# Gated attention and mixer: tokens permuted for longer reads, weights spread over batch 0, all score blocks of batch 0 computed, z doubled on chip

## The chip, the cores and the metric

The kernel runs on one core of one Trainium2 chip. The metric is the device time of one execution in microseconds (us). An execution is called fast or slow by its time against the fastest of the same kernel; all comparisons below are between fast runs. PE is the tensor engine, DVE the vector engine, ACT the scalar engine, POOL the GpSimd engine (it also issues the loads from memory here), and SP issues the DMA transposes and the stores. A line such as L116 is the line of the kernel that the profile belongs to; the same statement has another number in each kernel.

## The reference

Eight batches of 3008 tokens with 256 channels; z has 64 channels.

```python
scores = (1.0 / S) * np.matmul(z, z.transpose(0, 2, 1))
attn = np.maximum(scores, 0.0) ** 2
x = u * np.matmul(attn, v)                                   # first unit
h = np.maximum(x.transpose(0, 2, 1) @ w_tok1, 0.0) @ w_tok2  # second unit: mixer over tokens
y = x + h.transpose(0, 2, 1)
out = y + np.maximum(y @ w_ch1, 0.0) @ w_ch2                 # and over channels
```

## The kernel before

Tokens are cut in six blocks of 512 (the last has 448). For each batch there are six rows (blocks q of queries) of six groups (blocks g of keys): 36 groups. Scores are symmetric, so a block with g > q is computed once and transposed by a DMA ("flipped", tile `fl`) to serve as block (g, q). The mixer of a batch is cut in pieces that fill PE during the attention of the next batch; during batch 0 there are no such pieces, so batch 0 shows every wait.

Each engine runs its instructions in the order of the program. These are the parts that matter:

```python
def load_z(b, zT, c):            # two loads, one for each half of zr, then a transpose
    zr = sb.tile([P, GK, 2, d_qk], BF16, tag="zr", bufs=2)
    for h in range(2):
        nc.gpsimd.dma_start(out=zr[:, :t1 - t0, h, :], in_=z[b, t0 * P:t1 * P, :]
                            .rearrange("(t p) d -> p t d", p=P))
    ...                          # (the tail is cut)
    nc.sync.dma_start_transpose(out=zT[:, t0:t0 + GK, :], in_=...)

def load_uT(b, q):               # one load on POOL's queue, one transpose on SP's
    ...
# the start: z and v of batch 0, then
load_uT(0, 0)
load_weights()                   # all four weights in five DMAs
load_uT(0, 1)

def scores(b, q, g):
    ...                          # 4 matmuls; relu on ACT (rl), square on DVE (at, 3 buffers)
    if flip:                     # g > q
        fl = sb.tile([P, GK, QW], BF16, tag="fl", bufs=10)
        nc.sync.dma_start_transpose(out=fl..., in_=at[:])
        attn[b, g, q] = fl

for n, (b, q, g) in enumerate(groups):
    for f in fetch.get(n, []):   # loads put at group n
        f()
    if g >= q:
        scores(*directs[ahead])  # one computed block ahead
    ...                          # 8 matmuls of block g with v, gate with u at the end of the row
```

## Time and profile before

| stage (us from the start) | length | PE busy | granted clock |
|---|---|---|---|
| until the first scores, 0 to 9.4 | 9.4 | 0 | 1.00 |
| row 0 of batch 0, 9.4 to 74.5 | 65.1 | 22.1 | 0.90, 0.50, 0.79 |
| rows 1 to 5 of batch 0, 74.5 to 142.45 | 67.95 | 64.14 | 0.95 |
| batches 1 to 7 and the last mixer | 1123.95 | 1099.69 | 1.00 |

The whole is 1266.06 us (median of three runs, 1265.81 to 1267.21); the profiled span is 1266.4 us. The three clock figures of row 0 belong to its part before the empty stretch, to that stretch, and to its part after. The stages are told apart in the timeline of PE: a row begins with the 64-row matmuls of the tail block, which wait for the gate of the row before ("PE acc <- DVE xT"). The lines themselves are in the prediction.

### The profile page before, as it was taken

To read this page: it belongs to the slowest core of one execution; us is meant where nothing else is said; L and a number is where in the kernel's file an instruction comes from. 1 tells how busy PE (TensorE), PEld (TensorE's weight loads), DVE (VectorE), ACT (ScalarE), POOL (GpSimd) and SP (SyncE) were. 2 spreads that over 40 slices of the span, in tenths; PEclk is the share of its full clock that TensorE was granted. 3 is DMA by queue.
4 is the path that set the end of the run, shared out by engine and by line. 5 is a ranking of instruction groups with operands and counts; after the bars stand their busy time and mean duration, and the time that the engine had idled before them with its cause. 6 is when DMAs were issued, how large, how long until landed. Compare 5 with 4: busy or idle time off the path is not lost.

```text
span 1266.4 us, 17085 instructions
## 1 busy us (share of the span) xinstructions
PE 1185.9 (94%) x6929; PEld 623.5 (49%) x7008; DVE 578.1 (46%) x744; ACT 472.2 (37%) x489; POOL 174.7 (14%) x258
## 2 busy tenths in 40 slices
PE   4079989999999999999999999999999999999998
PEld 1023444555455645455455554555455554555566
DVE  1043355444644355534644436543554436444444
ACT  3044334334343144433434343432443334442122
POOL 7112301102120200203011020201102010000000
PEclk9589999999999999999999999999999999999999
DMA  9999998949798697959979497895979588553122
GB/s 114 196 183 174 167 151 144 157 81 173 130 146 148 97 169 136 151 104 138 168 123 159 92 166 137 139 164 87 174 124 163 100 138 148 111 116 84 32 74 67
DMA packets 560223, 168.60 MB, mean 133 GB/s; under 512 B 482384, under 2 KB 559632, under 8 KB 560144
## 3 DMA queue, kind: packets, MB, share of 16 engines
q1 hardware_dynamic: 453504, 131.64, 56.0%
q0 software_dynamic: 106640, 35.86, 26.9%
q8 instruction: 55, 0.90, 0.3%
q14 instruction: 24, 0.20, 0.1%
HBM read 71.70 MB, written 24.64 MB: 76 GB/s over the span
## 4 chain that ended last, share of the span: by engine, by line
PE 80%; DMA 7%; DVE 6%; issue 3%; ACT 2%; POOL 1%; SPq 0%; DVEq 0%; ACTq 0%; POOLq 0%
PE acc L212 34%; PE op L319 20%; PE hp L301 17%; PE sc L159 5%; DMA fl<-at 4%; PE a_ps L266 3%; DVE xT L284 3%; DMA ur<-in_u_dram 2%; ACT rl L172 2%; DVE h2pre L306 1%; DVE at L176 1%; DVE xT L238 1%; DMA zr<-in_z_dram 1%; DMA zT<-zr 0%; PE h_ps L280 0%
## 5 line engine op out<-in xcount | busy, mean ns | idle before, releaser
L172 ACT ACTIVATE rl<-sc 128x1024 bf16<-128x1024 f32 x336 | 324.2, 1016 | 451.8 <-PE sc L159 422.5
L212 PE MATMUL acc<-at,v_sb 128*128 128x512 bf16 (+1 forms) x1337 | 337.5, 385 | 45.3 <-DVE at L176 32.6
L212 PEld LDWEIGHTS <-v_sb 128*128 128x128 bf16 (+1 forms) x2304 | 210.2, 98 | 323.6 <-issue 123.8
L176 DVE TENSOR_TENSOR at<-rl 128x1024 bf16<-128x1024 bf16 x240 | 165.5, 692 | 271.7 <-ACT rl L172 206.6
L319 PE MATMUL op<-w_ch_sb,h2pre 128*128 128x256 bf16 (+1 forms) x2304 | 279.1, 273 | 1.1
L301 PE MATMUL hp<-xT,w_ch_sb 128*128 128x512 bf16 (+1 forms) x1120 | 272.0, 374 | 2.6 <-DVE xT L284 0.2
L319 PEld LDWEIGHTS <-h2pre 128*128 128x128 bf16 (+1 forms) x2304 | 224.2, 98 | 62.2 <-ACT h2pre L308 6.3
L308 ACT ACTIVATE h2pre<-hp 128x1024 bf16<-128x1024 f32 (+1 forms) x144 | 144.9, 1006 | 281.6 <-PE hp L301 263.9
L212 PE MATMUL acc<-fl,v_sb 128*128 128x512 bf16 (+1 forms) x921 | 223.8, 370 | 2.2 <-issue 0.2
L306 DVE TENSOR_SCALAR h2pre<-hp 128x1024 bf16<-128x1024 f32 (+1 forms) x144 | 172.6, 1200 | 79.6 <-PE hp L301 79.5
L301 PEld LDWEIGHTS <-w_ch_sb 128*128 128x128 bf16 x1152 | 112.6, 98 | 131.4 <-issue 4.4
L73 POOL DMA_DIRECT2D zr<-in_z_dram x96 | 72.3, 759 | 454.9 <-DMA zT<-zr 453.6
L327 DVE TENSOR_TENSOR res<-op,u_sb 128x512 f32<-128x512 f32 x88 | 60.7, 689 | 156.3 <-PE op L319 150.5
L159 PE MATMUL sc<-zT 64*128 64x512 bf16 (+1 forms) x672 | 105.4, 385 | 23.8 <-DMA zT<-zr 21.7
L178 DVE TENSOR_TENSOR at<-rl 128x1024 bf16<-128x1024 bf16 (+1 forms) x96 | 64.3, 680 | 76.5 <-ACT rl L172 71.1
L238 DVE TENSOR_TENSOR xT<-acc,uT 128x512 bf16<-128x512 f32 (+1 forms) x96 | 61.8, 665 | 71.7 <-PE acc L212 71.2
L88 POOL DMA_DIRECT2D v_sb<-in_v_dram x48 | 36.3, 762 | 366.3 <-PE acc L212 359.7
L159 PEld LDWEIGHTS <-zT 64*128 64x128 bf16 x672 | 20.5, 94 | 88.9 <-issue 60.5
L284 DVE TENSOR_TENSOR xT<-xT,h_ps 128x1024 bf16<-128x1024 bf16 (+1 forms) x48 | 53.9, 1193 | 22.4 <-PE h_ps L280 22.4
L100 POOL DMA_DIRECT2D ur<-in_u_dram x48 | 36.2, 754 | 69.0 <-DMA uT<-ur 65.9
L280 PE MATMUL h_ps<-w_tok_sb,a_sb 128*128 128x512 bf16 (+1 forms) x191 | 43.2, 374 | 1.6 <-ACT a_sb L272 0.7
L266 PE MATMUL a_ps<-x_sb,w_tok_sb 128*128 128x256 bf16 x384 | 44.4, 273 | 0.0
(21 smaller groups left out, 104.2 us busy)
## 6 DMA issues: line engine op xcount, KB each, us to landing
out_dram<-res SPq DMA_DIRECT2D x88, 256.0 KB, 2.5
v_sb<-in_v_dram POOLq DMA_DIRECT2D x40, 256.0 KB, 4.7
ur<-in_u_dram POOLq DMA_DIRECT2D x40, 256.0 KB, 5.5
zr<-in_z_dram POOLq DMA_DIRECT2D x80, 64.0 KB, 4.5
fl<-at SPq DMA_TRANSPOSE x120, 4.8
v_sb<-in_v_dram POOLq DMA_DIRECT2D x8, 192.0 KB, 8.2
w_ch_sb<-in_moe_w_ch_dram POOLq DMA_DIRECT2D x2, 768.0 KB, 26.1
ur<-in_u_dram POOLq DMA_DIRECT2D x8, 192.0 KB, 6.0
```

Of the source, the lines that this page charges most:

```text
L73: nc.gpsimd.dma_start(out=zr[:, : t1 - t0, h, :], in_=z[b, t0 * P:t1 * P, :].rearrange("(t p) d -> p t d", p=P))
L159: nc.tensor.matmul(sc[:, r, :W], zT[h, k * P:(k + 1) * P], zT[h, q * QW:q * QW + W], start=True, stop=True)
L172: nc.scalar.activation(rl[:, :, :W], sc[:, :, :W], ACT.Relu, scale=inv_S)
L176: nc.vector.tensor_mul(a4[:, :, pair, :], r4, r4)
L212: nc.tensor.matmul(o, vt[rows, i, dh * P:(dh + 1) * P], rhs, start=st, stop=sp, skip_group_check=True)
L238: nc.vector.tensor_mul(xT[:, dh, :full * P].rearrange("p (t s) -> p t s", s=P), acc[:, :full * P].rearrange("p (t s) -> p t s", s=P), uT[: ...
L266: nc.tensor.matmul(st["a_ps"][:, th, :], w_tok1_sb[:, k, th * P:(th + 1) * P], x[:, :, i, :], start=(k == 0 and th == 0), stop=(k == KT - ...
L284: nc.vector.tensor_add(xT[:, :, :W], xT[:, :, :W], h[:, :, :W])
L301: nc.tensor.matmul(hp[:, r, :W], w_ch1_sb[:, dc, cc * P:(cc + 1) * P], xT[:, dc, :W], start=(dc == 0), stop=(dc == DT - 1))
L306: nc.vector.tensor_single_scalar(h2[:, :, :W], hp[:, :, :W], 0.0, AX.max)
L308: nc.scalar.activation(h2[:, :, :W], hp[:, :, :W], ACT.Relu)
L319: nc.tensor.matmul(op[:rows[i], i, :], st["h2", q, cc // 2][:, cc % 2, c0:c0 + rows[i]], w_ch2_sb[:, cc, :], start=(cc == 0 and i == 0), s ...
```

## The change

Its intent: fewer and longer pieces in the loads (a partition reads four rows in one piece), no block of weights in front of u, no flips during batch 0 where DMA is the bottleneck, and half the loads of z. z of the later batches is also asked for later (from group 18 of the batch before theirs instead of from group 7) and doubled on POOL; this isn't printed here. The core of the change (comments and the changes of layout cut):

```diff
+    def rows_of(ap, c):
+        return ap[c * QW:c * QW + n * P, :].rearrange("(p t) d -> p t d", t=n)
-    def load_z(b, zT, c):  ...two loads into zr, transpose
+    def load_z(b, c):
+        zs = sb.tile([P, GK, d_qk], BF16, tag="zs", name="zs", bufs=6)
+        nc.gpsimd.dma_start(out=zs[:, :n, :], in_=rows_of(z[b], c))
+    def turn_z(zs, zT, c, engine):
+        zr = sb.tile([P, GK, 2, d_qk], BF16, tag="zr", name="zr", bufs=2)
+        engine.tensor_copy(zr[:], zs.unsqueeze(2).to_broadcast([P, GK, 2, d_qk]))
+        nc.sync.dma_start_transpose(out=zT[:, c * GK:c * GK + GK, :], in_=...)
 ...
+    def direct_block(b, q, g):
+        return b == 0 or g >= q
-        flip = g > q
+        flip = g > q and b > 0
 ...
-    load_uT(0, 0)
-    load_weights()
-    load_uT(0, 1)
+    for j, c in enumerate(vorder):
+        zs0[c] = load_z(0, c)
+        load_v(0, c)
+        if j == 2:
+            load_uT(0, 0)
 ...
+    at_group(4, lambda: load_uT(0, 1))
+    for c in range(NG):
+        at_group(NG + 1 + 4 * c, lambda c=c: load_w_tok1(c))
+        at_group(NG + 3 + 4 * c, lambda c=c: load_w_tok2(c))   # staged, reordered on POOL
+    for part in range(4):
+        at_group(2 * NG + 6 * part, lambda part=part: load_w_ch(part))
+    turn_z(zs0[vorder[0]], zTs[0], vorder[0], nc.vector)
     scores(*directs[0])
 ...
+        if n + 1 < NG:
+            c = groups[n + 1][2]
+            turn_z(zs0[c], zTs[0], c, nc.vector)
-        if g >= q and ahead < len(directs):
+        if direct_block(b, q, g) and ahead < len(directs):
             scores(*directs[ahead])
```

More of the change, by code (lines that the diff above doesn't have):

```diff
@@ L64, with last_rows @@
     w_ch2_sb = consts.tile([P, CHT, D], BF16)
-    def load_z(b, zT, c):
-        t0, t1 = c * GK, min(c * GK + GK, KT - 1)
-        zr = sb.tile([P, GK, 2, d_qk], BF16, tag="zr", name="zr", bufs=2)
-        for h in range(2):
-            nc.gpsimd.dma_start(
-                out=zr[:, : t1 - t0, h, :],
-                in_=z[b, t0 * P:t1 * P, :].rearrange("(t p) d -> p t d", p=P))
-        if t1 - t0 < GK:
+    full_tiles = [w // P for w in widths]
+    def rows_of(ap, c):
+        n = full_tiles[c]
+        return ap[c * QW:c * QW + n * P, :].rearrange("(p t) d -> p t d", t=n)
+    def last_rows(ap):
+        return ap[(KT - 1) * P:, :]
+    def load_z(b, c):
+        zs = sb.tile([P, GK, d_qk], BF16, tag="zs", name="zs", bufs=6)
+        n = full_tiles[c]
+        nc.gpsimd.dma_start(out=zs[:, :n, :], in_=rows_of(z[b], c))
+        if n < GK:
             for r in range(2):
                 nc.gpsimd.dma_start(
-                    out=zr[r * TAIL:(r + 1) * TAIL, GK - 1],
-                    in_=z[b, (KT - 1) * P:, :].unsqueeze(1)
-                    .to_broadcast([TAIL, 2, d_qk]))
+                    out=zs[r * TAIL:(r + 1) * TAIL, n, :], in_=last_rows(z[b]))
+        return zs
+    def turn_z(zs, zT, c, engine):
+        zr = sb.tile([P, GK, 2, d_qk], BF16, tag="zr", name="zr", bufs=2)
+        engine.tensor_copy(zr[:], zs.unsqueeze(2).to_broadcast([P, GK, 2, d_qk]))
         nc.sync.dma_start_transpose(
-            out=zT[:, t0:t0 + GK, :], in_=zr.rearrange("p t h d -> p (t h d)"))
+            out=zT[:, c * GK:c * GK + GK, :], in_=zr.rearrange("p t h d -> p (t h d)"))
     def load_v(b, c):
         vt = sb.tile([P, GK, D], BF16, tag="v", name="v_sb", bufs=8)
-        t0, t1 = c * GK, min(c * GK + GK, KT - 1)
-        nc.gpsimd.dma_start(
-            out=vt[:, : t1 - t0, :],
-            in_=v[b, t0 * P:t1 * P, :].rearrange("(t p) d -> p t d", p=P))
-        if t1 - t0 < GK:
+        n = full_tiles[c]
+        nc.gpsimd.dma_start(out=vt[:, :n, :], in_=rows_of(v[b], c))
+        if n < GK:
             for r in range(2):
                 nc.gpsimd.dma_start(
-                    out=vt[r * TAIL:(r + 1) * TAIL, GK - 1, :], in_=v[b, (KT - 1) * P:, :])
+                    out=vt[r * TAIL:(r + 1) * TAIL, n, :], in_=last_rows(v[b]))
         vs[b, c] = vt
@@ L98, in load_uT @@
         ur = sb.tile([P, QW // P, D], BF16, tag="ur", name="ur", bufs=2)
-        full, rest = widths[q] // P, widths[q] % P
-        nc.gpsimd.dma_start(
-            out=ur[:, :full, :],
-            in_=u[b, q * QW:q * QW + full * P, :].rearrange("(t p) d -> p t d", p=P))
-        if rest:
-            nc.gpsimd.memset(ur[rest:, full, :], 0.0)
-            nc.gpsimd.dma_start(
-                out=ur[:rest, full, :], in_=u[b, q * QW + full * P:q * QW + widths[q], :])
+        n = full_tiles[q]
+        nc.gpsimd.dma_start(out=ur[:, :n, :], in_=rows_of(u[b], q))
+        if n < QW // P:
+            nc.gpsimd.memset(ur[TAIL:, n, :], 0.0)
+            nc.gpsimd.dma_start(out=ur[:TAIL, n, :], in_=last_rows(u[b]))
         uT = sb.tile([P, QW // P, DT, P], BF16, tag="uT", name="uT", bufs=3)
@@ L111, in load_uT, with load_w_tok1 @@
         uTs[b, q] = uT
-    def load_weights():
-        nc.gpsimd.memset(w_tok1_sb[TAIL:, KT - 1, :], 0.0)
+    def load_w_tok1(c):
+        n = full_tiles[c]
         nc.gpsimd.dma_start(
-            out=w_tok1_sb[:, : KT - 1, :],
-            in_=moe_w_tok1[: (KT - 1) * P, :].rearrange("(t p) d -> p t d", p=P))
-        nc.gpsimd.dma_start(
-            out=w_tok1_sb[:TAIL, KT - 1, :], in_=moe_w_tok1[(KT - 1) * P:, :])
-        nc.gpsimd.dma_start(
-            out=w_tok2_sb[:], in_=moe_w_tok2.rearrange("(tc t) s -> t tc s", t=P))
-        nc.gpsimd.dma_start(
-            out=w_ch1_sb[:], in_=moe_w_ch1.rearrange("(dc d) c -> d dc c", d=P))
-        nc.gpsimd.dma_start(
-            out=w_ch2_sb[:], in_=moe_w_ch2.rearrange("(cc c) d -> c cc d", c=P))
+            out=w_tok1_sb[:, c * GK:c * GK + n, :], in_=rows_of(moe_w_tok1, c))
+        if n < GK:
+            nc.gpsimd.memset(w_tok1_sb[TAIL:, KT - 1, :], 0.0)
+            nc.gpsimd.dma_start(
+                out=w_tok1_sb[:TAIL, KT - 1, :], in_=last_rows(moe_w_tok1))
@@ new lines, in load_w_tok2 @@
+    def load_w_tok2(c):
+        st = sb.tile([P, DT, QW], BF16, tag="ws", name="ws", bufs=1)
+        W, n = widths[c], full_tiles[c]
+        nc.gpsimd.dma_start(
+            out=st[:, :, :W],
+            in_=moe_w_tok2.rearrange("(tc t) s -> t tc s", t=P)[:, :, c * QW:c * QW + W])
+        for h in range(DT):
+            nc.gpsimd.tensor_copy(
+                w_tok2_sb[:, h, c * QW:c * QW + n * P].rearrange("p (t s) -> p t s", s=P),
+                st[:, h, :n * P].rearrange("p (s t) -> p t s", t=n))
+        if n * P < W:
+            nc.gpsimd.tensor_copy(
+                w_tok2_sb[:, :, c * QW + n * P:c * QW + W], st[:, :, n * P:W])
@@ L130, with load_w_ch @@
+    def load_w_ch(part):
+        if part < 2:
+            nc.gpsimd.dma_start(
+                out=w_ch1_sb[:, part, :], in_=moe_w_ch1[part * P:(part + 1) * P, :])
+        else:
+            h = CHT // 2
+            c0 = (part - 2) * h
+            nc.gpsimd.dma_start(
+                out=w_ch2_sb[:, c0:c0 + h, :],
+                in_=moe_w_ch2.rearrange("(cc c) d -> c cc d", c=P)[:, c0:c0 + h, :])
     zTs, vs, uTs, xTs, xs = {}, {}, {}, {}, {}
     attn = {}
-    def key_order(q):
-        direct = list(range(q, NG))
+    def direct_block(b, q, g):
+        return b == 0 or g >= q
@@ L135, in key_order @@
+    def key_order(b, q):
+        direct = [g for g in range(NG) if direct_block(b, q, g)]
         if q == 0:
@@ L137, in key_order @@
         direct = [direct[-1]] + direct[:-1]
-        flipped = list(range(q))
+        flipped = [g for g in range(NG) if not direct_block(b, q, g)]
         order = []
@@ L145, in key_order @@
         return order
-    groups = [(b, q, g) for b in range(B) for q in range(NQ) for g in key_order(q)]
-    directs = [t for t in groups if t[2] >= t[1]]
+    groups = [(b, q, g) for b in range(B) for q in range(NQ) for g in key_order(b, q)]
+    directs = [t for t in groups if direct_block(*t)]
     def scores(b, q, g):
@@ L314, in ch2 @@
             us = st["u", q]
-            row0 = q * QW + half * 2 * P
-            rows = [min(P, S - row0 - j * P) for j in range(2)]
+            n = full_tiles[q]
+            rows = [P if half * 2 + j < n else TAIL for j in range(2)]
             c0 = (half * 2 + i) * P
@@ L331, in ch2 @@
                 nc.sync.dma_start(
-                    out=out[b, row0:row0 + 2 * P, :].rearrange("(i p) d -> p i d", p=P),
+                    out=rows_of(out[b], q)[:, half * 2:half * 2 + 2, :],
                     in_=res[:])
@@ L341, in ch2 @@
                     nc.sync.dma_start(
-                        out=out[b, row0 + j * P:row0 + j * P + r, :], in_=res[:r, j, :])
+                        out=rows_of(out[b], q)[:, half * 2 + j, :] if r == P
+                        else last_rows(out[b]), in_=res[:r, j, :])
         for q in range(NQ):
@@ L358, in new_zT, with at_group @@
         zTs[b] = sb.tile([P, KT, P], BF16, tag="zT", name="zT", bufs=2)
-    vorder = key_order(0)
+    vorder = key_order(0, 0)
     new_zT(0)
-    load_z(0, zTs[0], 0)
-    load_v(0, 0)
-    for c in vorder[1:]:
-        load_z(0, zTs[0], c)
+    zs0 = {}
+    for j, c in enumerate(vorder):
+        zs0[c] = load_z(0, c)
         load_v(0, c)
-    load_uT(0, 0)
-    load_weights()
-    load_uT(0, 1)
+        if j == 2:
+            load_uT(0, 0)
     fetch = {}
+    def at_group(n, f):
+        fetch.setdefault(n, []).append(f)
     for b in range(B):
@@ L377, with ask_z @@
             if m < B * NQ:
-                fetch.setdefault(base + q * NG + 2, []).append(
-                    lambda m=m: load_uT(m // NQ, m % NQ))
+                at_group(base + q * NG + 2, lambda m=m: load_uT(m // NQ, m % NQ))
         if b + 1 < B:
-            fetch.setdefault(base + NG, []).append(lambda b=b: new_zT(b + 1))
+            held = {}
+            def ask_z(b, c, held):
+                held[c] = load_z(b + 1, c)
+            at_group(base + 3 * NG, lambda b=b: new_zT(b + 1))
             for j, c in enumerate(vorder):
-                fetch.setdefault(base + NG + 1 + 3 * j, []).append(
-                    lambda b=b, c=c: load_z(b + 1, zTs[b + 1], c))
-                fetch.setdefault(base + (NQ - 1) * NG - 2 + (j if j > 1 else 0), []).append(
-                    lambda b=b, c=c: load_v(b + 1, c))
+                at_group(base + 3 * NG + j, lambda b=b, c=c, h=held: ask_z(b, c, h))
+                at_group(base + 3 * NG + j + 3, lambda b=b, c=c, h=held:
+                         turn_z(h.pop(c), zTs[b + 1], c, nc.gpsimd))
+                at_group(base + (NQ - 1) * NG - 2 + (j if j > 1 else 0),
+                         lambda b=b, c=c: load_v(b + 1, c))
+    at_group(4, lambda: load_uT(0, 1))
[4 more added lines that the diff above has]
+        at_group(2 * NG + 6 * part, lambda part=part: load_w_ch(part))
     queue = []
     per_batch = 0.87 * NQ * (2 + CHT // 2) + 1.35 * 4 * NQ
-    flat = NQ * NG * 1.73 + len(directs) / B * 0.63
+    flat = NQ * NG * 1.73 + NQ * (NQ + 1) / 2 * 0.63
     budget = 0.0
     ahead = 1
+    turn_z(zs0[vorder[0]], zTs[0], vorder[0], nc.vector)
     scores(*directs[0])
```

## The prediction

> **What bounds the kernel now.** I read, in this order, the page's slices, the totals by window, the chain of waits over the start, the list of waits, and the timeline of the first 150 us. First the slices (each digit is a fortieth of the span, 31.7 us, in tenths):
> ```profile
> PE   4079989999999999999999999999999999999998
> ...
> PEclk9589999999999999999999999999999999999999
> DMA  9999998949798697959979497895979588553122
> ```
> The tensor engine (PE) is nearly full from the third slice on. The loss is at the start: the second slice has no PE work and half the clock. Next the totals by window, cut where the timeline shows the phases to change (us; then busy us of PE, weight loads, DVE, ACT, POOL; granted clock; DMA share; GB/s):
> ```profile
> 9.40:36.80 27.40, 15.05 (x56) 4.06 (x57) 5.54 (x8) 10.05 (x11) 15.23 (x20) 0.90 1.24 135
> 36.80:64.50 27.70, 0.03 (x2) 0.06 (x1) 0.70 (x2) 0.67 (x1) 5.10 (x8) 0.50 1.25 197
> ...
> 74.50:142.45 67.95, 64.14 (x297) 24.36 (x300) 26.85 (x42) 27.20 (x30) 17.73 (x26) 0.95 1.19 171
> 142.45:1266.40 1123.95, 1099.69 (x6555) 592.91 (x6628) 541.16 (x688) 428.19 (x444) 128.94 (x190) 1.00 0.79 129
> ```
> Batch 0 has six rows of six groups (a group is 4 score matmuls, relu on ACT, square on DVE, 8 matmuls with v). Row 0 lasts from 9.4 to 74.5 and holds 27.7 us of nothing; rows 1 to 5 take 67.95 with PE busy 64.14; the other 1124 us, batches 1 to 7, have PE busy 1099.69, or 98%. Only the first 142 us have much to give. The chain of waits says what the empty 27.7 us were (start, length, what):
> ```profile
> 29.73 28.07 DMA ur<-in_u_dram
> 57.81 1.23 SPq L108
> 59.14 1.91 SPq L182
> 61.14 11.33 DMA fl<-at x2
> ```
> The u load for row 1 was issued after the weights, and landed 28 us later. SP stood at its transpose (L108), with the transposes of score blocks (fl, L182) behind it. The three at buffers could not be freed, so DVE, then ACT, then PE stopped. The list of waits agrees (total, times, longest):
> ```profile
> DVE at L176 <- DMA fl<-at: 57.0, 7, 39.2
> ...
> PE acc L212 <- DVE at L176: 32.6, 10, 27.7
> ```
> Last, the timeline of one group in row 0 and then of row 1 (PE, and below the dots ACT), start and length first:
> ```profile
> 9.39 1.03 PE L159 MATMUL sc<-zT 64*128 64x512 bf16 x4 [9.39 <-DMA zT<-zr]
> ...
> 12.01 0.69 DVE L178 TENSOR_TENSOR at<-rl 128x1024 bf16<-128x1024 bf16 x1 [0.22 <-ACT rl L172]
> ```
> ```profile
> 82.60 0.61 PE L159 MATMUL sc<-zT 64*128 64x512 bf16 x4
> 83.14 1.90 PE L212 MATMUL acc<-at,v_sb 128*128 128x512 bf16 x8
> 84.97 0.61 PE L159 MATMUL sc<-zT 64*128 64x512 bf16 x4
> ...
> 83.03 1.94 ACT L172 ACTIVATE rl<-sc 128x1024 bf16<-128x1024 f32 x2 [0.43 <-PE sc L159]
> ```
> Two things are to be seen. From zT landed to the group's last square is 12.01 + 0.69 - 9.39 = 3.31 us. And with data at hand, groups that all compute their scores follow each other every 84.97 - 82.60 = 2.37 us without a gap on PE, ACT idle 0.43 in each: PE bounds such groups.
>
> **What the Trainium skill says.** "DMA: Bandwidth & Descriptors", section "Anatomy of one DMA — SWDGE (gpsimd) path", says that a semaphore wait happens on the issuing sequencer before dispatch, not in the DMA engine. The trace agrees: SP's two L108 issues cover 28.74 us, and the fl issues come only after. This matters doubly below. "TensorE: Matmul & The Clock Gate", in "Why this matters for your kernels", says that gaps over about 3 us send the clock back to half; the trace agrees (0.50 in the stall, and four score matmuls take 1.03 us at 9.39 against 0.61 at 82.60). "VectorE: DVE Perf Modes", section "Side-by-side: where the cycles go for N=2048 bf16", gives about 150 cycles of start, 8 of fill and N/4 in the fastest mode of a one-source copy; the new copy of 512 elements would be (150 + 8 + 128)/0.96 GHz = 298 ns, an estimate from that page, as no such copy is in this trace. "SBUF — State Buffer", section "SBUF: two separate sides", says of the ports shared by DVE and GpSimd that whichever starts first holds the pair and the other blocks, also for a DVE op with two SBUF inputs against a GpSimd op that reads SBUF; the squares and POOL's new copies are such a pair, and no run here shows the cost yet.
>
> **The change, part by part.**
> (1) Batch 0 flips no blocks. This removes its 15 fl transposes and the stall of 27.7 us with the cold clock after it. It adds 15 score blocks in rows 1 to 5. PE issues one in 2.37 - 1.83 = 0.54 us (the 1.83 is from 83.14 to 84.97), 15 x 0.54 = 8.1 us. Now each such row is 6 x 2.37 = 14.2 plus about 1.0 at its border (the tail matmuls waited 0.77 + 0.23 us for the gate at 107.97), 15.2; the narrower row 5 is some 13.5. Sum 4 x 15.2 + 13.5 = 74.3, against 67.95 before: **+6.4 us**.
> (2) z is loaded once and doubled on DVE. Here I expect what eats most of the gain. The copy for group n+1 stands in DVE's program after the squares of group n, and zT for n+1 needs that copy. Thus in row 0 nothing of the next group may begin before the present group is squared. One turn of this ring: 3.31 (above) + 0.05 + 0.30 (copy) + 0.15 (to SP, chosen) + 2.6 to 3.0 (zT transpose, issue to landing: median 2.6 of the run, minimum 3.0 in the first 36 us) = 6.4 to 6.8, say **6.6 us a group**. Before, the six score groups of row 0 began at 9.4, 12.9, 18.4, 21.5, 26.8 and 35.8, so 5.3 apart.
> (3) Order on SP. u for row 0 is now asked for after three z and three v loads, and its transpose is SP's first instruction, ahead of every zT. POOL issues before it 3 z, 3 v (0.76 each) and 4 tails (0.6 each): 1.25 + 6 x 0.76 + 4 x 0.6 = 8.2, and u's issue ends at 9.0. It lands some 3.5 later (v took 3.1 to 5.5 from issue in this stretch), at 12.5; SP needs 1.3 for the issue (L108, 1.31), and zT, queued behind it, lands at about 17. So the first scores start near **17 instead of 9.4**.
> Row 0 then: scores of its last group at 17 + 5 x 6.6 = 50; squared at 53.3; the matmuls of this group, half of them after that and on a half-speed clock, and the gate take some 3.7 more: row 1 starts at about **57, against 74.5**: -17.5 us. The transposes of u for rows 2 and 1 stand on SP between zTs, but find it idle within the ring, so I add nothing.
> (4) Weights spread. They no longer hold u. As landed (bf16) batch 0 and the weights need 1.5 MB each for u, v and the two token weights, 1.5 for the channel weights, 0.4 for z, and 2.5 more for batch 1: some 10 MB within 115 us, 90 GB/s, and some 4 MB of transposes, 35 GB/s, together below the 171 to 197 GB/s of the windows above. I take it as hidden. The reorder of w_tok2 on POOL waits for its own load and holds POOL, but u for a row is asked for 15 groups ahead (7 for row 1): hidden too.
> (5) Longer pieces (z 1 KB read instead of 256 B, v and u 4 KB, out 2 KB). PE is 98% busy from 142.45 on, so only remnants can gain: DVE waited 4.9 us for fl there in all, and PE 3.6 for DVE. I take **-1 us**, for the start of batch 1 (one wait of 2.4 us at 162).
> Sum: -17.5 + 6.4 - 1 = -12; 1266 - 12 = **1254 us**.
>
> **The rivals.** (a) The intended outcome: row 0 runs as the loads come, at some 3 to 4 us a group; row 1 then starts at 35 to 40, the gain is 28 to 33 us, the time 1234 to 1238. For it: loads are no longer held by zr buffers, and in fewer pieces. Against: in-order DVE and SP make the ring above whatever the loads do. (b) Only the SP order is wrong, because u lands with z: first scores at 10 to 12, the time 1247 to 1249. (c) A new wait: POOL's copies share time with DVE squares, or the weights' loads (DMA share 1.19 already) delay u or zT in batch 0; each group of rows 1 to 5 that waits 0.3 us more costs 9 us, the time 1263, and more if zT of batch 1, now turned by POOL, holds SP and with it fl. For it: DMA was saturated there; against: fl, the largest mover, is gone, and POOL was busy for 175 us of 1266 only.
>
> **Range and chances.** The sum of 1254 has an error of some 5 us for the ring (six turns of ±0.5 us, and the first landing ±2) and some 5 for rows 1 to 5, with (b) on the low side and (c) on the high one: **1244 to 1263**. Faster by 2% means below 1240.7, which needs (a): **0.09**. Slower by 2% needs (c) in every batch: **0.02**. Within 2%: **0.89**.
>
> **What would show it.** In the profile of the changed kernel: SP's first issue is uT, and PE's first scores start at 15 to 19, not at 9; six score groups of row 0 stand 6 to 7 us apart, PE waiting for zT each time, and zT for DVE; row 1 starts at 53 to 61 with no empty slice; later groups of batch 0 are 2.37 us apart with PE full; batch 0 ends near 131 instead of 142; the rest takes 1121 to 1125. I am wrong if zT for the next group starts while DVE has not yet squared the present one, if rows 1 to 5 have waits of DVE for POOL or of the gate for u, or if the rest shortens by over 5 us: then the pieces of the transfers count for more than I gave them.

## The result, and the profile after

The changed kernel takes 1268.62 us (median of four runs, 1268.35 to 1269.89) against 1266.07 us (1265.81 to 1267.21). The ratio is 1.002 with a 95% interval of 1.0003 to 1.0038. A ratio is the mean time of one kernel's fast runs over that of the other's of the same rounds, so it is not quite the ratio of the medians. The time is the same, and it lies above the predicted range.

First the slices of the changed kernel, forty equal parts of the span:

```profile
PE   1399999999999999999999999999999999999998
...
PEclk9799999999999999999999999999999999999999
DMA  7656995679658697679956797577966788563122
```

The empty slice is gone: the second and third have 3 and 9 tenths instead of 0 and 7. The first is poorer, 1 tenth instead of 4. Then the totals by window, in the columns explained in the prediction (length; busy of PE, weight loads, DVE, ACT, POOL; clock; DMA share; GB/s), cut at the first scores, at the start of row 1, and at the start of batch 1:

```profile
0.00:21.80 21.80, 0.02 (x2) 0.02 (x4) 0.43 (x1) 1.28 (x1) 9.95 (x22) 1.00 0.93 132
21.80:69.37 47.57, 22.70 (x80) 6.45 (x81) 11.36 (x21) 14.52 (x16) 12.66 (x22) 0.78 0.63 99
69.37:145.57 76.20, 70.56 (x355) 24.31 (x360) 47.35 (x72) 57.17 (x62) 24.39 (x41) 1.00 0.69 99
145.57:1267.00 1121.43, 1099.44 (x6553) 592.86 (x6628) 544.80 (x688) 426.93 (x443) 100.89 (x192) 1.00 0.70 127
```

Row 1 starts at 69.37 instead of 74.5 (-5.1 us), rows 1 to 5 take 76.20 instead of 67.95 (+8.25), the rest takes 1121.43 instead of 1123.95 (-2.5). The sum is +0.6 us, the difference of the two spans. (The medians differ by 2.55 us: the profiled execution of the kernel before took 1268.15 us, 2.1 above its median, that of the changed kernel 1268.72, at its median. So the -2.5 of the rest may lie in that one execution.) So a stall of 27.7 us went away and row 0 became only 5 us shorter. The chain of waits says what came in its place (start, length, what):

```profile
7.05 6.68 DMA ur<-in_u_dram
13.75 7.53 DMA uT<-ur
...
25.32 2.47 DMA zT<-zr
...
31.38 2.44 DMA zT<-zr
...
37.19 5.06 DMA zT<-zr
...
45.84 5.93 DMA zT<-zr
...
55.36 5.69 DMA zT<-zr
```

Two things hold row 0. SP's first instruction is the transpose of u for row 0: it waits for u until 13.75, and u's transpose then takes 7.53 us. The first transpose of z is issued behind it, at 15.21, though its copy was made at 3.70, and the first scores wait for it until 21.78:

```profile
13.75 1.40 SPq L116 DMA_TRANSPOSE uT<-ur  x1
15.21 17.36 SPq L95 DMA_TRANSPOSE zT<-zr  x3
21.78 1.03 PE L191 MATMUL sc<-zT 64*128 64x512 bf16 x4 [21.78 <-DMA zT<-zr]
```

After that every block of z is transposed on the path itself, one after the other. The lines of the timeline between two of those transposes show the ring: the copy on DVE comes right after the second square, the transpose on SP when the copy is done (25.32 above), and the next scores start when it has landed.

```profile
24.40 0.69 DVE L210 TENSOR_TENSOR at<-rl 128x1024 bf16<-128x1024 bf16 x1 [0.22 <-ACT rl L204]
25.01 0.29 DVE L94 COPY zr<-zs 128x512 bf16<-128x512 bf16 x1
27.84 1.04 PE L191 MATMUL sc<-zT 64*128 64x512 bf16 x4 [5.02 <-DMA zT<-zr]
```

The chain view itself goes over POOL's next load of u between 21.3 and 25.0, but the copy doesn't read u; what it follows is the square.

The six score groups start at 21.78, 27.84, 33.87, 42.30, 51.81 and 61.10. The steps are 6.06, 6.03, 8.43, 9.51 and 9.29 us: the last three are longer because the transposes in them take 5 to 6 us instead of 2.4. POOL's lines of that time show what it had put on its queue:

```profile
22.33 0.54 POOL L123 DMA_DIRECT2D w_tok_sb<-in_moe_w_tok_dram  x1
36.29 0.53 POOL L111 DMA_DIRECT2D ur<-in_u_dram  x1 [13.42 <-DMA uT<-ur]
36.81 0.71 POOL L133 DMA_DIRECT2D ws<-in_moe_w_tok_dram  x1
```

The first weight piece was put at group 7, in row 1, and the piece at 36.81 at group 9; they were issued during groups 0 and 2. The other loads for w_tok2 (tile `ws`) followed at 44.10 and 54.27. POOL's copies out of this tile, which wait for the load, tell when each landed:

```profile
41.87 1.21 POOL L137 COPY w_tok_sb<-ws 128x512 bf16<-128x512 bf16 x2 [4.35 <-DMA ws<-in_moe_w_tok_dram]
51.25 1.22 POOL L137 COPY w_tok_sb<-ws 128x512 bf16<-128x512 bf16 x2 [6.42 <-DMA ws<-in_moe_w_tok_dram]
60.53 1.22 POOL L137 COPY w_tok_sb<-ws 128x512 bf16<-128x512 bf16 x2 [5.54 <-DMA ws<-in_moe_w_tok_dram]
```

The three slow transposes of z, each issued 0.4 to 1.7 us after such a load, ended at 42.25, 51.77 and 61.05, that is 0.4 to 0.5 us after it had landed. So here a transpose took about what was left of the load issued before it. No run tests this by itself. A place in the program gives POOL an order, not a time: POOL goes ahead until a semaphore holds it. From row 1 to the end of batch 0 the changed kernel behaves as predicted; in the timeline of PE, groups follow each other every 78.79 - 76.42 = 2.37 us without a gap:

```profile
76.42 0.61 PE L191 MATMUL sc<-zT 64*128 64x512 bf16 x4
76.95 1.90 PE L244 MATMUL acc<-at,v_sb 128*128 128x512 bf16 x8
78.79 0.60 PE L191 MATMUL sc<-zT 64*128 64x512 bf16 x4
```

### The profile page after: what moved, and what is told of

Its sections match the earlier page's. It is cut to its first block, busy times and chain, and to the rows that moved or that the text cites. A ratio compares the mean times of both kernels' runs of the same rounds, so it can differ in the third digit from the quotient of the medians.

```text
span 1267.0 us, 17239 instructions
## 1 busy us (share of the span) xinstructions
PE 1192.7 (94%) x6986; PEld 623.6 (49%) x7068; DVE 603.9 (48%) x780; ACT 499.9 (39%) x519; POOL 147.9 (12%) x277
## 4 chain that ended last, share of the span: by engine, by line
PE 83%; DVE 6%; DMA 4%; issue 3%; ACT 2%; POOL 0%; DVEq 0%; ACTq 0%; POOLq 0%
PE acc L244 36%; PE op L351 20%; PE hp L333 17%; PE sc L191 7%; PE a_ps L298 3%; DVE xT L316 3%; ACT rl L204 2%; DMA zT<-zr 2%; DVE h2pre L338 1%; DVE xT L270 1%; DVE at L208 1%; DMA ur<-in_u_dram 1%; DMA fl<-at 1%; DMA uT<-ur 1%; PE h_ps L312 0%
## 5 line engine op out<-in xcount | busy, mean ns | idle before, releaser
L204 ACT ACTIVATE rl<-sc 128x1024 bf16<-128x1024 f32 (+1 forms) x366 | 351.8, 1014 | 424.3 <-PE sc L191 424.3
L244 PE MATMUL acc<-at,v_sb 128*128 128x512 bf16 (+2 forms) x1450 | 361.7, 382 | 14.9 <-DVE xT L270 11.8
L208 DVE TENSOR_TENSOR at<-rl 128x1024 bf16<-128x1024 bf16 x210 | 147.7, 705 | 188.3 <-ACT rl L204 188.2
L244 PE MATMUL acc<-fl,v_sb 128*128 128x512 bf16 (+1 forms) x805 | 197.3, 370 | 1.8
L210 DVE TENSOR_TENSOR at<-rl 128x1024 bf16<-128x1024 bf16 (+1 forms) x156 | 107.7, 699 | 143.1 <-ACT rl L204 139.3
L191 PE MATMUL sc<-zT 64*128 64x512 bf16 (+1 forms) x732 | 114.8, 386 | 47.8 <-DMA zT<-zr 45.7
L94 POOL COPY zr<-zs 128x512 bf16<-128x512 bf16 x42 | 28.8, 685 | 494.6 <-DMA zT<-zr 494.3
L316 DVE TENSOR_TENSOR xT<-xT,h_ps 128x1024 bf16<-128x1024 bf16 (+1 forms) x48 | 53.9, 1193 | 19.5 <-PE h_ps L312 19.5
L111 POOL DMA_DIRECT2D ur<-in_u_dram x48 | 25.9, 541 | 246.2 <-DMA uT<-ur 244.1
L101 POOL DMA_DIRECT2D v_sb<-in_v_dram x48 | 26.0, 543 | 144.2 <-PE acc L244 143.4
```

What stands on the lines that cost most here:

```text
L191: nc.tensor.matmul(sc[:, r, :W], zT[h, k * P:(k + 1) * P], zT[h, q * QW:q * QW + W], start=True, stop=True)
L204: nc.scalar.activation(rl[:, :, :W], sc[:, :, :W], ACT.Relu, scale=inv_S)
L208: nc.vector.tensor_mul(a4[:, :, pair, :], r4, r4)
L210: nc.vector.tensor_mul(a3[:, pair, :W], rl[:, :, :W], rl[:, :, :W])
L244: nc.tensor.matmul(o, vt[rows, i, dh * P:(dh + 1) * P], rhs, start=st, stop=sp, skip_group_check=True)
L316: nc.vector.tensor_add(xT[:, :, :W], xT[:, :, :W], h[:, :, :W])
```

## The experiments

The theory (A): row 0 is held by the ring square, copy, transpose, scores, by SP's order, and by loads that lengthen the transposes in flight. The rival (B): row 0 is bound by the loads, and ring and order only show it. All times are medians; "row 1" is the start of row 1 in the profiled run, "rows 1 to 5" and "rest" as above. Each call of runs had its own runs of the kernel before on the same chip: 1266.94 us for the first four, 1267.27 for the next four, 1266.19 for the last three. Some kernels spread: e6_before_u from 1272.93 to 1286.56 us with a profile of 1285.74, e8_all_flips from 1260.49 to 1268.83, e11_before_spread from 1270.78 to 1278.51. The stages are those of the one profiled execution.

| run | us | ratio to before (95%) | row 1 | rows 1 to 5 | rest |
|---|---|---|---|---|---|
| kernel before | 1266.07 | 1 | 74.51 | 67.9 | 1124.0 |
| changed kernel | 1268.62 | 1.002 (1.0003 to 1.0038) | 69.37 | 76.2 | 1121.4 |
| e1_ring | 1243.76 | 0.9816 (0.98 to 0.9832) | 40.71 | 76.6 | 1124.7 |
| e2_order | 1261.92 | 0.9958 (0.9942 to 0.9974) | 61.22 | 76.6 | 1122.2 |
| e3_hold | 1266.17 | 0.9995 (0.9976 to 1.0013) | 58.39 | 76.2 | 1129.1 |
| e4_flips | 1282.80 | 1.0125 (1.0108 to 1.0141) | 73.22 | 68.4 | 1138.9 |
| e5_noperm | 1268.21 | 1.0011 (0.9996 to 1.0026) | 68.36 | 76.3 | 1121.2 |
| e6_before_u | 1280.37 | 1.0104 (1.0051 to 1.0157) | 87.55 | 73.5 | 1122.9 |
| e7_all | 1239.47 | 0.9786 (0.9768 to 0.9804) | 35.25 | 77.0 | 1124.0 |
| e8_all_flips | 1267.19 | 0.9985 (0.9952 to 1.0018) | 43.12 | 91.3 | 1132.7 |
| e9_turn_dve | 1268.85 | 1.0014 (0.9997 to 1.003) | 69.41 | 77.0 | 1121.1 |
| e10_paced | 1235.42 | 0.9752 (0.9737 to 0.9766) | 31.20 | 76.7 | 1126.3 |
| e11_before_spread | 1274.75 | 1.0061 (1.0033 to 1.0088) | 63.84 | 85.6 | 1125.3 |

All outputs are right.

### The ring cut

```diff
-        zr = sb.tile([P, GK, 2, d_qk], BF16, tag="zr", name="zr", bufs=2)
+        zr = sb.tile([P, GK, 2, d_qk], BF16, tag="zr", name="zr", bufs=6)
 ...
-    turn_z(zs0[vorder[0]], zTs[0], vorder[0], nc.vector)
+    for c in vorder:
+        turn_z(zs0[c], zTs[0], c, nc.vector)
     scores(*directs[0])
 ...
-        if n + 1 < NG:
-            c = groups[n + 1][2]
-            turn_z(zs0[c], zTs[0], c, nc.vector)
```

> Changed kernel with only the ring of row 0 cut: six zr buffers, and DVE doubles all six z blocks before the first squares; everything else, also u's transpose first on SP, as in the change. Theory A (the serial ring square -> copy -> transpose -> scores costs row 0 its time): first scores stay near 21.8 us, the six score groups then stand 2.4 to 3.5 us apart instead of 6.0 to 9.5, row 1 starts at 38 to 46 instead of 69.4, time 1240 to 1246. Theory B (row 0 is bound by the loads themselves, the ring only shows it): the groups stay 5 us or more apart and the time stays above 1258.

Measured: 1243.76 us, row 1 at 40.71. The first scores start at 21.56, and in the timeline of PE the later groups of row 0 now stand 2.3 to 2.4 us apart:

```profile
27.58 0.72 PE L191 MATMUL sc<-zT 64*128 64x512 bf16 x4
29.84 0.61 PE L191 MATMUL sc<-zT 64*128 64x512 bf16 x4
32.23 0.61 PE L191 MATMUL sc<-zT 64*128 64x512 bf16 x4
```

The loads are the same and row 0 is 28.7 us shorter, so B falls for this part: the loads did not bind row 0, the ring did. (The buffers and the place of the copies were changed together. The time fell by 24.9 us, as the rest grew by 3.3.)

### The order on SP

The load of u for row 0 stays where it is; its transpose is emitted at group 1, after two z transposes.

```diff
         if j == 2:
-            load_uT(0, 0)
+            ask_u(0, 0)                 # the load only
 ...
+    fetch.setdefault(1, []).insert(0, lambda: turn_u(0, 0))   # the transpose
```

> Changed kernel with only the place of the first u transpose on SP moved: u is loaded at the same point, but its transpose is issued after the transposes of the first two z blocks. Theory A: first scores at 7 to 9 us instead of 21.8; the steps of the ring that fall among v's loads take 6 to 8 us, later ones as before, so row 1 starts 8 to 13 us earlier and the time is 1256 to 1261. Rival (the ring is paced by the loads, so an earlier start is given back): time within 3 us of the changed kernel's 1268.6.

Measured: 1261.92 us, row 1 at 61.22; the first scores start at 9.96 instead of 21.78. Of the 11.8 us won there, 3.7 are given back inside the ring: the second z transpose now takes 6.33 us beside v's loads. The rival's "within 3 us" falls (-6.7), and theory A's time was 1 us too low. The order is worth some 7 us here. Weight loads are again in flight with the later transposes, which take 3.8 to 5.4 us.

### The weights held until row 0 is done

```diff
+    def hold():
+        w = sb.tile([P, 2], BF16, tag="hold", name="hold", bufs=1)
+        nc.gpsimd.tensor_copy(w[:], xTs[0, 0][:, DT - 1, :2])
+    at_group(NG, hold)
     for c in range(NG):
         at_group(NG + 1 + 4 * c, lambda c=c: load_w_tok1(c))
```

> Changed kernel with one two-element copy on POOL added, which reads the gated output of row 0, so that POOL starts the weights and later loads only after row 0. Theory A (the last three steps of the ring, 8.4 to 9.5 us, were lengthened by the weights' loads in flight): all five steps are near 6.05 us, row 1 starts 8 to 10 us earlier, at 59 to 62 us, time 1258 to 1262, if the later loads still come in time. Rival (the transposes are slow for another reason, such as the two u transposes between them on SP): the steps keep their 8.4 to 9.5 us, the time stays at 1266 to 1271.

Measured: 1266.17 us, row 1 at 58.39. Every transpose of the ring now takes 2.4 us; these are the last three in the chain of waits, to be held against 5.06, 5.93 and 5.69 in the changed kernel:

```profile
35.88 2.41 DMA zT<-zr
...
41.67 2.42 DMA zT<-zr
...
47.46 2.42 DMA zT<-zr
```

The two u transposes are still between them on SP, so these are not the cause; the loads in flight are (the weights, and u for row 3 behind the same hold). With no load in flight these two, at 31.10 and 42.90, took 3.1 us each from issue to landing; the one for row 0, beside v's loads, took 7.44 in the same run. With the loads held back the steps are 5.8 to 6.1 us. But the time fell by 2.5 us only, not by the 11 us of row 0: the same loads then came late. POOL could use the last piece of w_tok2 at 130.49 us instead of 135.15, under five us earlier, while batch 1 began eleven us earlier, and the rest grew by 7.7 us; at the start of batch 1 DVE waited up to 10.3 us for fl and PE 2.0 us for x, both transposes. The bytes had to go somewhere. My expected time missed this.

### The flips of batch 0 restored

```diff
-        return b == 0 or g >= q
+        return g >= q
 ...
-        flip = g > q and b > 0
+        flip = g > q
```

> Changed kernel with only part 1 undone: batch 0 again flips its 15 blocks by transposes. Rows 1 to 5 lose 8.1 us of score matmuls. Theory A: in row 0 the flipped blocks' transposes go to SP between the z transposes and sit in the ring, 4 to 5 us for each of five, so row 0 ends 10 to 20 us later and the time is 1270 to 1281; that would say that part 1 bought something only because of the ring. Rival (the flips are free beside the ring): time 1259 to 1263.

Measured: 1282.80 us, 14 us worse. My mechanism was only partly right. Row 0 ended 3.9 us later, not 10 to 20. Rows 1 to 5 won 7.8 us, the score matmuls that part 1 had added. The loss, 17.5 us, came in the rest: POOL was held by the transposes and asked for v of batch 1 and the last weights late, so that at the start of batch 1 PE waited three times for v (7.1 us) and 5.4 us for x. The waits at these places fit the reading that flips in batch 0 take DMA time that the weights need.

### The permutation undone

The layout is `(t p)` again, so z is read in pieces of 256 B and v and u of 1 KB, and w_tok2 is loaded without POOL's reorder:

```diff
-        return ap[c * QW:c * QW + n * P, :].rearrange("(p t) d -> p t d", t=n)
+        return ap[c * QW:c * QW + n * P, :].rearrange("(t p) d -> p t d", p=P)
```

> Changed kernel with only the permutation undone (tokens 128 apart in a partition, so z is read in pieces of 256 B, v and u of 1 KB; the token weights loaded straight, without POOL's reorder). Theory A (the slow z transposes of row 0 come from loads in flight, however they are cut): steps of the ring in row 0 of 6 to 9.5 us as in the changed kernel or longer; the rest after batch 0 grows by the 1 to 3 us that it had shrunk by; time 1268 to 1276. Rival (it is the long pieces that slow the transposes): the last three steps fall to 6 to 7 us and the time to 1258 to 1263.

Measured: 1268.21 us, and the changed kernel 1268.62: the permutation is worth nothing that this can see. The last five transposes of the ring sum to 2.81 + 2.44 + 6.54 + 2.41 + 6.54 = 20.7 us, against 21.6 with long pieces, so it is not the length of the pieces that slows a transpose. The rest is 1121.2, as short as with the permutation, against my expectation; if the 2.5 us there were won at all, they come from something else, which no run isolates. The edit also removes POOL's reorder, so the two could in principle offset each other.

### The kernel before with u ahead of the weights

```diff
     load_uT(0, 0)
-    load_weights()
     load_uT(0, 1)
 ...
+    fetch.setdefault(3, []).append(load_weights)
```

> Kernel before with one thing moved: the weights are asked for after u of row 2, instead of before u of row 1. Theory A (the 27.7 us without work in the kernel before were nothing but u for row 1 behind the weights on POOL's queue): the empty stretch goes, row 1 starts at 45 to 54 us instead of 74.5, some of it given back where the weights now collide with the block transposes in rows 1 and 2; time 1238 to 1250. Rival (the DMA engines are saturated by 5 MB of weights wherever they stand): the stall only moves, time above 1258.

Measured: 1280.37 us (1272.93 to 1286.56): a clear miss of mine, and the rival's time (above 1258) is right. The stall moved. On SP four block transposes now span 54 us, and PE stood still from 53.1 to 87.55:

```profile
43.61 54.40 SPq L182 DMA_TRANSPOSE fl<-at  x4
```

In the kernel before, the weights landed while SP stood at u and PE had nothing to do. The 27.7 us were thus not a misplaced wait alone: they were also the time in which 4.6 MB of weights (counted as bf16) landed without block transposes in their way.

### The kernel before with the weights spread only

Part 4 alone: the weights in the same pieces at the same groups as in the changed kernel, all else as before.

```diff
-    load_weights()
 ...
+    for c in range(NG):
+        fetch.setdefault(NG + 1 + 4 * c, []).append(lambda c=c: load_w_tok1(c))
+        fetch.setdefault(NG + 3 + 4 * c, []).append(lambda c=c: load_w_tok2(c))
+    for part in range(4):
+        fetch.setdefault(2 * NG + 6 * part, []).append(lambda part=part: load_w_ch(part))
```

> Kernel before with only part 4 of the change: the weights cut in pieces and spread over batch 0 at the same groups as in the changed kernel; tokens, z and the flipped blocks as before. From the two runs with flips in batch 0, whose block transposes waited for each other beside the loads: row 1 starts at 48 to 58 instead of 74.5, but rows 1 to 5 take 80 to 95 us instead of 68, time 1253 to 1270. If the spread alone had been enough: rows 1 to 5 at 68 to 72, time 1240 to 1248.

Measured: 1274.75 us, 0.6% slower than before and above my range. Rows 1 to 5 took 85.6 us, as expected, and row 1 started at 63.84, later than expected. Spread at these groups, the weights are no gain while batch 0 flips.

### Three repairs together

All z before v, the ring cut, and u's transpose after the z blocks:

```diff
-    for j, c in enumerate(vorder):
+    for c in vorder:
         zs0[c] = load_z(0, c)
+    for j, c in enumerate(vorder):
         load_v(0, c)
 ...                                     # and the edits of e1_ring and e2_order
```

> Changed kernel with three repairs together: all z blocks asked for before v, all six doubled before the first squares (six zr buffers), and u of row 0 transposed on SP after the z blocks. Theory A: first scores at 7 to 9 us, groups of row 0 then 2.4 to 4 us apart, paced by v landing, row 1 starts at 25 to 31 us, batch 0 ends near 103, time 1226 to 1233. If the loads bind row 0 instead: row 1 at 36 or later, time above 1238.

Measured: 1239.47 us, below both kernels (whether by 2% is unclear: the ratio's interval is 0.9768 to 0.9804), and 6 us short of my range; by its time it is the other expectation, loads that bind row 0, that came true. Row 1 starts at 35.25, not at 25 to 31: the first four score groups start at 9.29, 14.55, 19.05 and 24.39, with z's transposes waiting beside v's loads (issue to landing 12.2 us in the median, for six in a queue).

### The three repairs, with flips restored

The edits of e7_all and of e4_flips.

> As the run with the three repairs, and also part 1 undone: batch 0 flips 15 blocks by transposes again. If the ring was all that made flips dear, this is up to 8 us faster than computing all blocks (8.1 us of score matmuls less): 1219 to 1227. If the block transposes collide with the loads and with u on SP, as in the kernel before, it is equal or slower: 1229 to 1242.

Measured: 1267.19 us. With the ring gone, part 1 is worth 27.7 us. I had allowed for a collision and put it at 1242 at the most. Row 0 ends 7.9 us later than with all blocks computed, rows 1 to 5 take 14.3 us more in spite of 8.1 us fewer score matmuls, and the rest 8.7 us more. The block transposes, issue to landing (minimum, median, maximum, us), first in the kernel before from row 1 into batch 1 (14 of them from 72 us on, all weights landed by 57), then in batch 0 of this run (15), then in the run with u ahead of the weights (4, from 43.6 us on):

```profile
DMA to landing us min/median/max: 4.4/6.2/9.2
```

```profile
DMA to landing us min/median/max: 4.3/9.0/16.1
```

```profile
DMA to landing us min/median/max: 7.3/19.5/41.9
```

The medians go the way of the weights in flight with them, but the three windows differ in other things too. Part 4 did not pay without part 1; part 1 without part 4 was not run.

### z of later batches doubled on DVE

```diff
-                         turn_z(h.pop(c), zTs[b + 1], c, nc.gpsimd))
+                         turn_z(h.pop(c), zTs[b + 1], c, nc.vector))
```

> Changed kernel with z of batches 1 to 7 doubled on DVE instead of POOL (42 copies of 512 elements a partition). If the port shared by POOL's copies and DVE's squares costs the end of the chain anything, this gains 1 to 4 us; if the squares have slack there, it stays within 2 us of the changed kernel (1267 to 1270); if DVE in its order now waits for z, it loses 2 to 10 us.

Measured: 1268.85 us, as the changed kernel. POOL's copies and DVE's squares do meet, as this pair of lines from the run with three repairs shows (two squares took 2.04 us beside two POOL copies, 1.28 alone), but no time is lost by it here:

```profile
35.51 1.69 POOL L147 COPY w_tok_sb<-ws 128x512 bf16<-128x512 bf16 x2 [6.00 <-DMA ws<-in_moe_w_tok_dram]
35.72 2.04 DVE L220 TENSOR_TENSOR at<-rl 128x1024 bf16<-128x1024 bf16 x2
```

### v of row 0 paced

The edits of e7_all, and POOL waits for z's third and fifth transpose before it asks for more of v:

```diff
     for j, c in enumerate(vorder):
+        if j in (2, 4):
+            hold(j)                     # a two-element copy that reads zT of block j
         load_v(0, c)
-        if j == 2:
-            ask_u(0, 0)
+    ask_u(0, 0)
```

> The run with three repairs, and v of row 0 paced: POOL asks for the third and fourth v block only after the third z transpose, for the last two after the fifth (by two-element copies that read zT), and for u of row 0 at the end. Theory (with three repairs, row 0 was held by z transposes that took 4.5 to 5.3 us each beside v's loads): z transposes land 1.3 to 2.5 us apart from 7 us on, groups of row 0 stand 2.4 to 3.5 us apart, row 1 starts at 26 to 31 instead of 35.25, time 1231 to 1236. Rival (v is then what comes late, one for one): row 1 stays at 33 to 38, time 1237 to 1242.

Measured: 1235.42 us, the fastest of all, 2.5% below the kernel before. Row 1 starts at 31.20. The first three score groups start at 9.14, 13.17 and 17.67, the next at 20.34 and 22.71, already at the pace of PE. So v's loads had held the transposes, and asking for v later brought it early enough. (The load of u for row 0 was moved behind v as well; its share isn't told apart.)

## Why the prediction was wrong

**What was right.** The reading of the stall in the kernel before; that the copy stands behind the squares on DVE and makes a ring of row 0; that u's transpose, first on SP, delays the first scores; that groups of rows 1 to 5 stand 2.37 us apart; that most of the gain would be eaten. The copy took 0.29 us against an estimated 0.30. Rows 1 to 5 took 76.2 us against 74.3.

**The step that failed** is part 4, "I take it as hidden". I compared mean rates over the whole of batch 0 and concluded that the weights fit. But the ring has a transpose on its path at every turn, and what a transpose takes depends on what is in flight with it at that time. The weights placed in row 1 were issued during row 0, as POOL goes ahead of PE. With them in flight the last three transposes took 5.1 to 5.9 us; with them held back, 2.4. The same oversight is in part 3: from u landed, at 12.5, I allowed 4.5 us until the first zT, and it took 8.0 (13.75 to 21.78). There u's transpose took 7.53 beside v's loads, and with no load in flight, in the run that holds the weights, 3.1.

The sum by these terms: row 1 started at 69.4 instead of the predicted 57, 12.4 us late. The first scores came at 21.8 instead of 17 (4.8 us), the five steps of the ring took 39.3 instead of 33 (6.3 us), and the end of row 0 took 8.3 instead of 7 (1.3 us). Rows 1 to 5 added 1.9 us. The rest was 1121.4 where the prediction had 1123, 1.6 us to the good. Together 12.4 + 1.9 - 1.6 = 12.7 us above 1254, which is the measured 1267 of the profiled span. With the weights held row 1 started at 58.39, near the predicted 57, but then the same loads came beside batch 1, and the rest grew by 7.7 us; so they weren't hidden there either. Without the loads the ring turned in 5.8 to 6.1 us, a little faster than my 6.6.

**The rivals.** (a), row 0 as the loads come, was wrong for this kernel, but it is what it becomes once the ring is cut: 1243.76, 1239.47 and 1235.42 us. (c) had the right suspicion, loads that delay zT, but placed it in rows 1 to 5 and thought of POOL's copies; the runs without them (those for z on DVE, those for w_tok2 left out) kept the same time. For part 5 I gave 1 us; the run without the permutation shows none.

**Where the expected gain went.** The wait of 27.7 us was the time in which the weights landed. In the changed kernel they land during row 0 and rows 1 to 5, which is possible because batch 0 no longer flips. But row 0 was made serial at the same time, and 28.7 us were lost to that, as the run with the ring cut shows. (The 11 us of the weights are no further loss to be added: once the ring is cut, the later groups of row 0 run at PE's pace with the same loads in flight.) That the two are of the same size, so that the time came out the same, is chance. What stays open is whether the rest is 2.5 us shorter at all, and by what rule a transpose shares the DMA engines with loads.

## What to carry to other kernels

When a small copy is put between a load and its transpose, look at what stands ahead of it on its engine: behind work that depends on the previous transpose it closes a ring, and a prefetch becomes a chain. A load's place in the program orders a queue and does not pace it; an engine that has nothing to wait for issues it long before. Do not price a DMA on the critical path at its median of the whole run: price it with what will be in flight beside it (the three slow transposes here ended just after the load issued before them), and test a "hidden" load by holding it back for the stage in question.

## What the Trainium skill lacked or had wrong

- "DMA: Bandwidth & Descriptors" gives a bandwidth for a DMA transpose ("Latency and other measured facts") and says that a DMA engine takes turns between the queues that have work for it ("Queues, rings and completion order"), but no figure for a transpose beside plain loads. Here a 128 KB z transpose took 2.4 us alone and 5.1 to 5.9 beside weight loads; a 256 KB u transpose 3.1 alone and 7.5 beside v's loads; and a 512 KB block transpose 6.2, 9.0 or 19.5 us in the median, with no weights in flight, with the weights spread, and with all of them asked for at once.
- The same page calls descriptor generation on the gpsimd path "small, variable" ("Anatomy of one DMA — SWDGE (gpsimd) path") and gives no figure by the number of pieces. In these runs POOL's issue of a load that has four pieces in a partition took 0.76 us, and 0.54 us with one piece, on the engine that issues all loads.
- The same page ("Specifications") gives 512 B as the least transfer for line rate. No run here tests it: reading z in pieces of 256 B instead of 1 KB, and v and u in 1 KB instead of 4 KB, left the time at 1268.2 us, against 1268.6, in a kernel that these loads didn't bind.
- Nothing lacking, but seen: "SBUF — State Buffer" ("SBUF: two separate sides") states the lock between a GpSimd operation that reads SBUF and a DVE operation with two SBUF inputs. The trace agrees (two squares 2.04 us instead of 1.28 beside POOL copies); taking z's copies off POOL left the time at 1268.85 us, against 1268.62.
